# Linear attention and a swish layer on one core: the tail chunk moves from last place to last but one

## The chip, the cores and the metric

The kernel runs on one core of a Trainium2 chip. The core has five engines with instruction streams of their own: TensorE (PE, matrix products, with its weight loads shown as PEld), VectorE (DVE), ScalarE (ACT), GpSimd (POOL) and SyncE (SP, which here only issues transfers). Sixteen DMA engines move data between the memory outside the core (HBM) and the on-chip memory of 128 partitions. The metric is the device time of one execution in microseconds. Before the change it was 293.87 us, the median of three runs from 293.31 to 294.41.

## The reference, cut to what matters

```python
q_s = softmax(q, axis=-1)              # over the 64 elements of a head
k_s = softmax(k, axis=2)               # over the 576 tokens of a batch
kv  = einsum('bhsd,bhse->bhde', k_s, v)
x   = einsum('bhsd,bhde->bhse', q_s, kv)   # then (b, s) rows of h*d = 512
h   = x @ w_in                         # 4608x512 by 512x2048
g   = h * (1 / (1 + exp(-beta * h)))
out = g @ w_out                        # 4608x2048 by 2048x512, float32
```

There are 8 batches, 8 heads, 576 tokens and 64 elements per head. The two products of the second half are most of the arithmetic.

## The kernel before, in words

The 4608 rows are worked in nine chunks of 512 rows. Chunks 0 to 7 hold the first 512 tokens of each batch ("main"), four tokens in each partition. Chunk 8 (`c == B`) holds what is left, the last 64 tokens of all eight batches ("tail"); its partitions 0 to 63 belong to even batches and 64 to 127 to odd ones.

For each chunk a loop runs over `j`, the sixteen blocks of 128 columns of the hidden layer. `mm_a` (L309) makes one block of h with four products and lets ACT take a tanh (L326) and DVE form g (L328). `mm_b` (L340) multiplies g into four accumulators, one for each block `st` of 128 rows, with a lag of two blocks. The accumulators of a chunk are finished in the first two steps of the next chunk (`finish_b`, L431), where `store` (L356) copies them to a staging tile of four buffers (`wo`), ACT the even and DVE the odd ones, and issues the stores to HBM. A main chunk in mid-kernel is stored by two transfers on SP, each of two row blocks on all 128 partitions, 4 KB in a row (L378).

What the next chunk needs is prepared beside this one. `side(c, u)` (L538) is called at each step `u` and, for `b = c + 1`, emits q's exponential, sum and scaling (steps 2 to 5), k's exponential and v's cast (steps 4 to 6), the transpose of the scaled q by a DMA on SP (`q_xbar`, step 6, L235), the k-by-v products and their normalization (steps 8 and 10) and the products that make x (`x_mm`, steps 11 to 14). For a main chunk `x_mm` is one product of 512 columns for each of four head pairs; for the tail chunk it is eight products of 64 columns for each (L300). At step 9 `load_next` (L423) issues on SP the loads of the chunk after next: q (L80), k (L104, with its 64 tail tokens at L108) and v (likewise). The tail chunk needs only q, which `load_qtail` (L83) fetches with eight transfers of 64 partitions and 256-byte rows (L88).

The order on each engine is that of the program: the kernel is scheduled by hand. So SP's queue has, in each chunk, two stores, a transpose, and then the loads, and an instruction that waits holds what follows it.

In the last chunk the sixteenth block is drained in another order (L585 to L590): accumulators 0 and 1 are finished first, then 2, then 3, and each is stored as soon as it is ready. Because the last chunk is the tail, each store is cut in two halves of 64 partitions (`e` = 0 and 1): blocks 0 and 1 together by two transfers on SP, block 2 by two on ACT, block 3 by one on SP and one on ACT.

```python
(nc.scalar if st == 2 or (st == 3 and e) else nc.sync).dma_start(   # L367
```

Of the kernel before, what the change touches and what calls it, by code (L numbers as in the profile page):

```python
# [10 lines left out]
F32 = mybir.dt.float32  # L11
# [6 lines left out]
def kernel(  # L18
# [10 lines left out]
    nc = tc.nc  # L29
# [6 lines left out]
    NJ = FF // P  # L36
# [5 lines left out]
    NW = 2  # L42
    D1 = D + 1
    LAG = 2
    NCH = B + 1

    const = ctx.enter_context(tc.tile_pool(name="const", bufs=1))
    stage = ctx.enter_context(tc.tile_pool(name="stage", bufs=1))
# [26 lines left out]
    def load_q(b, parts=1):  # L75
        t = stage.tile([P, H, R * D], F32, tag="q_st", bufs=2, name=f"q_st{b}")
        src = q[b, :, 0:MAIN, :].rearrange("h (p i) d -> p h (i d)", i=R)
        n = H // parts
        for s in range(parts):
            nc.sync.dma_start(t[:, s * n : (s + 1) * n, :], src[:, s * n : (s + 1) * n, :])  # L80
        q_st[b] = t
# [12 lines left out]
    def load_kv(d, src, b, tag, parts=1):  # L94
        t = stage.tile([P, H * (R + 1) * D], F32, tag=tag, bufs=2, name=f"{tag}{b}")
        if b < NW:
            d[b] = t[:, 0 : HP * RW * D].rearrange("p (j r) -> p j r", j=HP)
            sv = src[b].rearrange("(j e) (p i) d -> (e p) j (i d)", e=2, i=RW)
            n = HP // parts
            for s in range(parts):  # L100
                nc.sync.dma_start(d[b][:, s * n : (s + 1) * n, :], sv[:, s * n : (s + 1) * n, :])
        else:
            d[b] = t[:].rearrange("p (h r) -> p h r", h=H)
            nc.sync.dma_start(  # L104
                d[b][:, :, 0 : R * D], src[b, :, 0:MAIN, :].rearrange("h (p i) d -> p h (i d)", i=R)
            )
            e = b % 2
            nc.sync.dma_start(  # L108
                d[b][e * TAIL : (e + 1) * TAIL, :, R * D : R * D + D],
                src[b, :, MAIN:S, :].rearrange("h t d -> t h d"),  # L110
            )
# [140 lines left out]
    def kv_mm(b, jj, n=2, tag="att"):  # L252
        t = ps.tile([P, n, 2 * D1], F32, tag=tag, bufs=2 if tag == "att" else 1, name=f"kv{b}_{jj}")
        att_of[b, jj] = t
        for jl in range(n):
            j = n * jj + jl
            if b < NW:
                for i in range(RW):
                    nc.tensor.matmul(
                        t[:, jl, 0:D1],  # L260
                        ek[b][:, j, i, :],
                        va[b][:, j, i, :],
                        start=(i == 0),
                        stop=(i == RW - 1),
                    )
                continue
            for i in range(R):
# [14 lines left out]

    def kv_norm(b, jj, n=2):
        t = att_of.pop((b, jj))
        rk = work.tile([P, n, 1], F32, tag="rk", bufs=2, name=f"rk{b}_{jj}")
        nc.vector.reciprocal(rk[:], t[:, :, D : D + 1])
        for e in range(2):
            r = slice(e * D, (e + 1) * D)
            dst = kvp[r, b, n * jj : n * jj + n, e * D : (e + 1) * D]
            src = t[r, :, 0:D] if b < NW else t[r, :, e * D1 : e * D1 + D]  # L290
# [49 lines left out]
    def mm_b(c, j, sts=range(R)):  # L340
        acc = acc_tiles(c)
        g = g_of[c, j]
        for st in sts:
            nc.tensor.matmul(  # L344
                acc[st][:],
                g[:, ds(st * P, P)],
                w_out_b[:, j, :],
                start=(j == 0),
                stop=(j == NJ - 1),
            )  # L350
# [5 lines left out]
    def store(c, st):  # L356
        acc = acc_of[c]
        eng = nc.scalar if st % 2 == 0 else nc.vector
        if c == B:
            lo, hi = ((0, 2), (0, 2), (2, 3), (3, 4))[st]  # L360
            if st == lo:
                o_of[c] = stage.tile([P, R, DM], F32, tag="wo", bufs=4, name=f"o{c}_{lo}")
            o = o_of[c]
            evac(eng, o[:, st, :], acc[st][:])
            if st == hi - 1:
                for e in range(2):
                    (nc.scalar if st == 2 or (st == 3 and e) else nc.sync).dma_start(  # L367
                        out_t[:, MAIN:S, :].rearrange("(i e) t f -> e t i f", e=2)[e, :, lo:hi, :],
                        o[e * TAIL : (e + 1) * TAIL, lo:hi, :],
                    )  # L370
            return
        if st == 0:
            o_of[c] = stage.tile([P, R, DM], F32, tag="wo", bufs=4, name=f"o{c}")
        o = o_of[c]
        evac(eng, o[:, st, :], acc[st][:])
        if st % 2 == 1:
            ov = out[c * S : c * S + MAIN, :].rearrange("(p i) f -> p i f", i=R)
            nc.sync.dma_start(ov[:, st - 1 : st + 1, :], o[:, st - 1 : st + 1, :])  # L378
# [41 lines left out]
    ek_buf(1, nc.gpsimd)  # L420
    v_buf(1)

    def load_next(nb):  # L423
        if nb < B:
            load_q(nb)
            load_kv(k_st, k, nb, "k_st")
            load_kv(v_st, v, nb, "v_st")
        elif nb == B:
            load_qtail()

    def finish_b(c, j):  # L431
        mm_b(c, j)
# [67 lines left out]
    pool_cast(("in", 3), ("out", 3))  # L500

    for u in range(4, NJ):
        mm_a(0, u)
# [7 lines left out]
        if u in (11, 13):  # L511
# [23 lines left out]
    mm_b(1, 0)  # L535
    mm_b(1, 1)

    def side(c, u):  # L538
        b = c + 1
        if b > B:  # L540
            return
        tail = b == B
        o = 2 if c == 1 else 0
        if u in (2 + o, 3 + o):
            q_exp(b, u - 2 - o)
            q_sum(b, u - 2 - o)
        if u in (4 + o, 5 + o):
            q_mul(b, u - 4 - o)
            if not tail:
                k_exp(b, u - 4 - o)  # L550
        if u == 4 + o and not tail:
            v_buf(b)
            v_cast(b, nc.gpsimd)
            vtail_cast(b, nc.gpsimd)
        if u == 6 + o:
            if not tail:
                ktail_exp(b)
            q_xbar(b)
        if u in (8 + o, 10 + o) and not tail:
            kv_mm(b, (u - 8 - o) // 2)  # L560
            kv_norm(b, (u - 8 - o) // 2)
        if 11 <= u < 15:
            j = u - 11
            x_mm(b, j, nc.scalar if j % 2 == 0 else nc.vector)
        if u == 9:
            load_next(c + 2)

    for u in range(4):
        side(1, u)
    for c in range(1, NCH):  # L570
        for j in range(4 if c == 1 else 0, NJ - 1 if c == B else NJ):
            lead = c > 1 and j == 3
            if not lead:
                mm_a(c, j)
            if c > 1 and j == 2:
                mm_a(c, 3)
            if (c, j) == (B, NJ - 2):
                pass
            elif j >= LAG:
                mm_b(c, j - LAG)  # L580
            else:
                finish_b(c - 1, NJ + j - LAG)
            side(c, j)
    mm_a(B, NJ - 1, tag="att")
    last = [(0, j) for j in range(NJ - 4, NJ - 1)] + [(1, j) for j in range(NJ - 4, NJ - 1)]  # L585
    last += [(0, NJ - 1), (1, NJ - 1)] + [(st, j) for st in (2, 3) for j in range(NJ - 4, NJ)]
    for st, j in last:
        mm_b(B, j, [st])
        if j == NJ - 1:
            store(B, st)  # L590
# [1 line left out]
_INS = ['q', 'k', 'v', 'moe_w_in', 'moe_w_out', 'moe_beta']  # L592
_OUTS = [((4608, 512), 'float32')]
# [25 lines left out]
```

The softmax here doesn't subtract the row's maximum and nothing guards it: scores larger than these inputs give would overflow.

## Time and profile before

| What | Value |
|---|---|
| Median of three runs | 293.87 us |
| The profiled execution's own time | 294.54 us |
| Its span, first to last instruction | 292.4 us |
| PE busy | 279.5 us, 96% |
| DVE busy | 184.2 us, 63% |
| ACT busy | 163.9 us, 56% |
| POOL busy | 42.0 us, 14% |
| Granted TensorE clock | 0.996 |

The profile is one execution. Its span leaves out 2.1 us of the execution's own time, which lie before the first or after the last instruction. Lines of the timeline read: start in us from the span's start, duration in us, engine, source line, operation, output and inputs, number of instructions merged. A trailing q on an engine's name (SPq, ACTq) means that the engine's queue was issuing a transfer. "To landing" is the time from the issue of a transfer to the arrival of its last byte as the profile sees it. The lines of the stretch views give the stretch, its length, the busy time and instruction count of PE, PEld, DVE, ACT and POOL, the granted clock, the mean busy share of the sixteen DMA engines, and the GB/s that they moved.

### The profile page before, as it was taken

How to read it: one execution, taken by the hardware profiler on the slowest of the kernel's cores; microseconds unless marked ns; L12 is line 12 of the kernel's file. 1: busy time of each engine (PE TensorE's matmuls, PEld its weight loads, DVE VectorE, ACT ScalarE, POOL GpSimd, SP SyncE). 2: the span in 40 equal slices, each digit the busy share in tenths (PEclk: the TensorE clock that was granted, in tenths of full speed). 3: DMA queues.
4: the chain of work that ended last, by engine and by line, in shares of the span. 5: the costliest groups of instructions: out<-in, count | busy, mean ns of one | idle time of the engine just before them, and what ended most of it. 6: DMA issues, size and time to landing. Idle time of an engine off the chain costs nothing.

```text
span 292.4 us, 3879 instructions
## 1 busy us (share of the span) xinstructions
PE 279.5 (96%) x1447; PEld 131.0 (45%) x1475; DVE 184.2 (63%) x299; ACT 163.9 (56%) x238; POOL 42.0 (14%) x55
## 2 busy tenths in 40 slices
PE   8898979999999999999999999999999999999991
PEld 3443435445444444454445444544454444544440
DVE  7853696695578557855695469456954694563441
ACT  4863666684486448734773567346825654453340
POOL 4539670300030021002100110003000000000000
PEclk9999999999999999999999999999999999999998
DMA  7999999708932963297319821981293023012005
GB/s 243 378 385 371 377 385 311 248 2 233 296 152 62 315 162 123 62 326 177 123 40 302 223 90 54 303 234 64 84 165 52 32 115 72 0 58 87 0 0 144
DMA packets 55971, 50.06 MB, mean 171 GB/s; under 512 B 26241, under 2 KB 47761, under 8 KB 55953
## 3 DMA queue, kind: packets, MB, share of 16 engines
q1 hardware_dynamic: 55712, 49.43, 55.8%
q10 hardware_dynamic: 240, 0.39, 0.5%
q8 instruction: 11, 0.18, 0.3%
q14 instruction: 8, 0.06, 0.1%
HBM read 36.71 MB, written 9.44 MB: 158 GB/s over the span
## 4 chain that ended last, share of the span: by engine, by line
PE 85%; DMA 6%; DVE 2%; ACT 1%; issue 1%; SPq 1%; another core or an unknown queue 1%; POOL 0%; ACTq 0%
DMA w_out_100<-in_moe_w_out_dram 4%; DMA v_st_91<-in_v_dram 2%; PE acc_3_724 L344 1%; PE acc_2_2458 L344 1%; PE acc_0_2456 L344 1%; PE acc_3_2459 L344 1%; PE acc_1_2167 L344 1%; PE acc_1_1300 L344 1%; PE acc_1_1589 L344 1%; PE acc_1_2728 L344 1%; PE acc_1_1011 L344 1%; PE acc_1_722 L344 1%; PE acc_1_1878 L344 1%; PE acc_2_1879 L344 1%; PE acc_2_1590 L344 1%; PE acc_0_721 L344 1%
## 5 line engine op out<-in xcount | busy, mean ns | idle before, releaser
L316 PEld LDWEIGHTS <-w_in_b 128*128 128x128 bf16 x576 | 55.3, 98 | 65.5 <-issue 2.7
L386 PEld LDWEIGHTS <-kvp 128*128 128x128 bf16 x34 | 3.7, 117 | 6.2 <-issue 3.6
L140 POOL CAST va_2202<-v_st_2007 128x2048 bf16<-128x2048 f32 x1 | 1.9, 1919 | 29.5 <-DMA v_st_2007<-in_v_dram 29.5
L140 POOL CAST va_1913<-v_st_1718 128x2048 bf16<-128x2048 f32 x1 | 1.9, 1918 | 26.7 <-DMA v_st_1718<-in_v_dram 26.7
L140 POOL CAST va_1624<-v_st_1429 128x2048 bf16<-128x2048 f32 x1 | 1.9, 1922 | 26.6 <-DMA v_st_1429<-in_v_dram 26.6
L153 ACT ACTIVATE ek_144<-k_st_86 64x576 bf16<-64x576 f32 x8 | 5.5, 681 | 0.2
L153 ACT ACTIVATE ek_149<-k_st_118 64x576 bf16<-64x576 f32 x8 | 5.4, 676 | 0.0
L140 POOL CAST va_1046<-v_st_836 128x2048 bf16<-128x2048 f32 x1 | 1.9, 1920 | 24.0 <-DMA v_st_836<-in_v_dram 24.0
L140 POOL CAST va_1335<-v_st_1140 128x2048 bf16<-128x2048 f32 x1 | 1.9, 1917 | 22.7 <-DMA v_st_1140<-in_v_dram 22.7
L296 PEld LDWEIGHTS <-kvp 128*128 128x128 bf16 x32 | 3.1, 98 | 4.2 <-DVE kvp L291 1.0
L140 POOL CAST va_147<-v_st_91 128x576 bf16<-128x576 f32 x4 | 3.3, 860 | 6.3 <-DMA v_st_91<-in_v_dram 6.3
L209 ACT ACTIVATE eq_189<-q_st_83 128x1024 bf16<-128x1024 f32 x2 | 2.1, 1056 | 3.0 <-DMA q_st_83<-in_q_dram 3.0
L140 POOL CAST va_783<-v_st_132 128x2048 bf16<-128x2048 f32 x1 | 1.9, 1916 | 12.2 <-DMA v_st_132<-in_v_dram 12.2
L140 POOL CAST w_in_b<-w_in_114 128x1024 bf16<-128x1024 f32 x2 | 3.0, 1536 | 2.1 <-DMA w_in_114<-in_moe_w_in_dram 2.1
L226 DVE TENSOR_TENSOR eq_485<-eq_485,rq_487 128x1024 bf16<-128x1024 bf16 x2 | 3.3, 1652 | 0.0
L140 POOL CAST w_out_b<-w_out_100 128x1024 bf16<-128x1024 f32 x2 | 2.4, 1205 | 4.6 <-DMA w_out_100<-in_moe_w_out_dram 4.6
L140 POOL CAST w_out_b<-w_out_116 128x1024 bf16<-128x1024 f32 x2 | 2.6, 1292 | 1.7 <-DMA w_out_116<-in_moe_w_out_dram 1.7
L220 DVE TENSOR_REDUCE rq_191<-eq_189 128x16 f32<-128x1024 bf16 x2 | 2.4, 1215 | 0.3 <-ACT eq_189 L209 0.3
L220 DVE TENSOR_REDUCE rq_487<-eq_485 128x16 f32<-128x1024 bf16 x2 | 2.4, 1212 | 0.3 <-ACT eq_485 L209 0.3
L220 DVE TENSOR_REDUCE rq_748<-eq_746 128x16 f32<-128x1024 bf16 x2 | 2.4, 1212 | 0.3 <-ACT eq_746 L209 0.3
L220 DVE TENSOR_REDUCE rq_1887<-eq_1885 128x16 f32<-128x1024 bf16 x2 | 2.4, 1191 | 0.3 <-ACT eq_1885 L209 0.3
L220 DVE TENSOR_REDUCE rq_2176<-eq_2174 128x16 f32<-128x1024 bf16 x2 | 2.4, 1190 | 0.3 <-ACT eq_2174 L209 0.3
(1461 smaller groups left out, 838.9 us busy)
## 6 DMA issues: line engine op xcount, KB each, us to landing
k_st_86<-in_k_dram SPq DMA_DIRECT2D x4, 288.0 KB, 5.7
v_st_91<-in_v_dram SPq DMA_DIRECT2D x4, 288.0 KB, 6.5
k_st_118<-in_k_dram SPq DMA_DIRECT2D x4, 288.0 KB, 9.6
v_st_124<-in_v_dram SPq DMA_DIRECT2D x2, 576.0 KB, 9.3
q_st_83<-in_q_dram SPq DMA_DIRECT2D x2, 512.0 KB, 4.3
w_in_97<-in_moe_w_in_dram SPq DMA_DIRECT2D x2, 512.0 KB, 6.4
w_out_100<-in_moe_w_out_dram SPq DMA_DIRECT2D x2, 512.0 KB, 9.3
w_in_102<-in_moe_w_in_dram SPq DMA_DIRECT2D x1, 1024.0 KB, 9.3
```

Of the source, the lines that this page charges most:

```text
L140: eng.tensor_copy(dst, src)
L153: nc.scalar.activation(ek[b][r, j : j + m, :, e * D : (e + 1) * D], k_st[b][r, j : j + m, :].rearrange("p j (i d) -> p j i d", i=RW), ACTF ...
L209: nc.scalar.activation(eq[b][:, :, s * m : (s + 1) * m, :].rearrange("p i h d -> p h i d"), q_st[b][:, s * m : (s + 1) * m, :].rearrange(" ...
L220: nc.vector.tensor_reduce(rq[b][:, 0, :, h], eq[b][:, :, h, :], axis=AX.X, op=ALU.add)
L226: nc.vector.tensor_tensor(eq[b][:, :, h, :], eq[b][:, :, h, :], rq[b][:, 1, :, h].unsqueeze(3).to_broadcast((P, R, m, D)), ALU.mult,)
L296: nc.tensor.matmul(t[:], kvp[:, c, j, :], qsT[c][:, :, j, :])
L316: nc.tensor.matmul(h[:], w_in_b[:, kt, ds(j * P, P)], x_of(c)[:, kt, :], start=(kt == 0), stop=(kt == KT - 1),)
L344: nc.tensor.matmul(acc[st][:], g[:, ds(st * P, P)], w_out_b[:, j, :], start=(j == 0), stop=(j == NJ - 1),)
L386: nc.tensor.matmul(t[:, 0:cols], kvp[:, B - 1, 0, :], kvp[:, B - 1, :, :].rearrange("p j r -> p (j r)")[:, 0:cols],)
```

## The change

The chunks get an explicit order. With `LASTMAIN` set, the tail chunk runs in the eighth place and the main chunk of batch 7 in the ninth. `side` now takes a place `n`: q and x are prepared for the chunk in place n + 1, k and v still for batch n + 1. So in place 6 (chunk 6) the tail's q is worked together with k and v of batch 7, and in place 7 (the tail chunk) q of batch 7 is worked alone. `load_next` follows: the tail's eight loads are issued in place 5, ahead of k and v of batch 7, and q of batch 7 in place 6. The tail chunk is stored in mid-kernel by four transfers of 64 partitions on SP. The last chunk, now a main one, uses four staging tiles and four stores of 128 partitions and one row block each: blocks 0, 2 and 3 on SP, block 1 on ACT. Two other switches of the new text, `FIX` and `COLT`, are off.

```diff
-    NCH = B + 1
+    FIX, LASTMAIN, COLT = False, True, False
+    NCH = B + 1
+    order = list(range(NCH))
+    if LASTMAIN:
+        order[B - 1], order[B] = B, B - 1
+    LASTC = order[-1]
...
     def store(c, st):
         acc = acc_of[c]
         eng = nc.scalar if st % 2 == 0 else nc.vector
+        if c == B and c != LASTC:
+            if st == 0:
+                o_of[c] = stage.tile([P, R, DM], F32, tag="wo", bufs=4, name=f"o{c}")
+            o = o_of[c]
+            evac(eng, o[:, st, :], acc[st][:])
+            if st % 2 == 1:
+                for e in range(2):
+                    nc.sync.dma_start(
+                        out_t[:, MAIN:S, :].rearrange("(i e) t f -> e t i f", e=2)[e, :, st - 1 : st + 1, :],
+                        o[e * TAIL : (e + 1) * TAIL, st - 1 : st + 1, :],
+                    )
+            return
...
+        if c == LASTC:
+            o = stage.tile([P, R, DM], F32, tag="wo", bufs=4, name=f"o{c}_{st}")
+            evac(eng, o[:, st, :], acc[st][:])
+            ov = out[c * S : c * S + MAIN, :].rearrange("(p i) f -> p i f", i=R)
+            (nc.sync, nc.scalar, nc.sync, nc.sync)[st].dma_start(ov[:, st, :], o[:, st, :])
+            return
...
-    def load_next(nb):
-        if nb < B:
-            load_q(nb)
-            load_kv(k_st, k, nb, "k_st")
-            load_kv(v_st, v, nb, "v_st")
-        elif nb == B:
+    def load_next(n):
+        if order[n] < B:
+            load_q(order[n])
+        else:
             load_qtail()
+        if n < B:
+            load_kv(k_st, k, n, "k_st")
+            load_kv(v_st, v, n, "v_st")
...
-    def side(c, u):
-        b = c + 1
-        if b > B:
+    def side(n, u):
+        if n + 1 >= NCH:
             return
-        tail = b == B
+        qc = order[n + 1]
+        kb = n + 1
...
-            q_exp(b, u - 2 - o)
-            q_sum(b, u - 2 - o)
+            q_exp(qc, u - 2 - o)
+            q_sum(qc, u - 2 - o)
...
-            x_mm(b, j, nc.scalar if j % 2 == 0 else nc.vector)
-        if u == 9:
-            load_next(c + 2)
+            x_mm(qc, j, nc.scalar if j % 2 == 0 else nc.vector)
+        if u == 9 and n + 2 < NCH:
+            load_next(n + 2)
...
-    for c in range(1, NCH):
-        for j in range(4 if c == 1 else 0, NJ - 1 if c == B else NJ):
+    for n in range(1, NCH):
+        c = order[n]
+        for j in range(4 if n == 1 else 0, NJ - 1 if n == B else NJ):
...
-        mm_b(B, j, [st])
+        mm_b(LASTC, j, [st])
         if j == NJ - 1:
-            store(B, st)
+            store(LASTC, st)
```

More of the change, by code (lines that the diff above doesn't have):

```diff
@@ L266, in kv_mm @@
                 continue
+            if COLT:
+                for i in range(R + 1):
+                    for e in range(2):
+                        hd = 2 * j + e
+                        nc.tensor.matmul(
+                            t[e * D : (e + 1) * D, jl, 0:D1],
+                            ek[b][:, i, hd, :] if i < R else ekt[(b // 2) % 2][:, ds(hd * D, D)],
+                            va[b][:, i, hd, :] if i < R else vt[(b // 2) % 2][:, b % 2, hd, :],
+                            start=(i == 0),
+                            stop=(i == R),
+                            tile_position=(0, e * D),
+                        )
+                continue
             for i in range(R):
@@ L289, in kv_norm @@
             dst = kvp[r, b, n * jj : n * jj + n, e * D : (e + 1) * D]
-            src = t[r, :, 0:D] if b < NW else t[r, :, e * D1 : e * D1 + D]
+            src = t[r, :, 0:D] if b < NW or COLT else t[r, :, e * D1 : e * D1 + D]
             nc.vector.tensor_tensor(dst, src, rk[r].to_broadcast((D, n, D)), ALU.mult)
@@ L358, in store @@
         eng = nc.scalar if st % 2 == 0 else nc.vector
+        if c == B and c != LASTC:
[4 more added lines that the diff above has]
+            if st % 2 == 1:
+                for e in range(2):
+                    nc.sync.dma_start(
+                        out_t[:, MAIN:S, :].rearrange("(i e) t f -> e t i f", e=2)[e, :, st - 1 : st + 1, :],
+                        o[e * TAIL : (e + 1) * TAIL, st - 1 : st + 1, :],
+                    )
+            return
         if c == B:
@@ L366, in store @@
                 for e in range(2):
-                    (nc.scalar if st == 2 or (st == 3 and e) else nc.sync).dma_start(
+                    if FIX:
+                        q_eng = (nc.sync, nc.sync, nc.gpsimd, nc.scalar if e else nc.sync)[st]
+                    else:
+                        q_eng = nc.scalar if st == 2 or (st == 3 and e) else nc.sync
+                    q_eng.dma_start(
                         out_t[:, MAIN:S, :].rearrange("(i e) t f -> e t i f", e=2)[e, :, lo:hi, :],
@@ L421 @@
     v_buf(1)
-    def load_next(nb):
-        if nb < B:
-            load_q(nb)
-            load_kv(k_st, k, nb, "k_st")
-            load_kv(v_st, v, nb, "v_st")
-        elif nb == B:
+    def load_next(n):
+        if order[n] < B:
+            load_q(order[n])
+        else:
             load_qtail()
+        if n < B:
+            load_kv(k_st, k, n, "k_st")
+            load_kv(v_st, v, n, "v_st")
     def finish_b(c, j):
@@ L502 @@
     for u in range(4, NJ):
-        mm_a(0, u)
+        if not (FIX and u == 5):
+            mm_a(0, u)
+        if FIX and u == 4:
+            mm_a(0, 5)
+            mm_b(0, 2)
+            continue
+        if FIX and u in (12, 14):
+            for j in (u - 12, u - 11):
+                q_pet(1, j, nc.scalar if u == 12 else nc.vector)
         mm_b(0, u - LAG)
@@ L510 @@
             q_mul(1, (u - 10) // 2)
-        if u in (11, 13):
+        if not FIX and u in (11, 13):
             for j in (u - 11, u - 10):
@@ L536 @@
     mm_b(1, 1)
-    def side(c, u):
-        b = c + 1
-        if b > B:
+    def side(n, u):
+        if n + 1 >= NCH:
             return
-        tail = b == B
-        o = 2 if c == 1 else 0
+        qc = order[n + 1]
+        kb = n + 1
+        o = 2 if n == 1 else 0
         if u in (2 + o, 3 + o):
-            q_exp(b, u - 2 - o)
-            q_sum(b, u - 2 - o)
+            q_exp(qc, u - 2 - o)
+            q_sum(qc, u - 2 - o)
         if u in (4 + o, 5 + o):
[L548 to L554, printed above, removed]
-        if u == 6 + o:
[L556 to L561, printed above, removed]
+            q_mul(qc, u - 4 - o)
+            if kb < B:
+                k_exp(kb, u - 4 - o)
+        if u == 4 + o and kb < B:
+            v_buf(kb)
+            v_cast(kb, nc.gpsimd)
+            vtail_cast(kb, nc.gpsimd)
+        if u == 6 + o:
+            if kb < B:
+                ktail_exp(kb)
+            q_xbar(qc)
+        if u in (8 + o, 10 + o) and kb < B:
+            kv_mm(kb, (u - 8 - o) // 2)
+            kv_norm(kb, (u - 8 - o) // 2)
         if 11 <= u < 15:
             j = u - 11
-            x_mm(b, j, nc.scalar if j % 2 == 0 else nc.vector)
-        if u == 9:
-            load_next(c + 2)
+            x_mm(qc, j, nc.scalar if j % 2 == 0 else nc.vector)
+        if u == 9 and n + 2 < NCH:
+            load_next(n + 2)
     for u in range(4):
         side(1, u)
-    for c in range(1, NCH):
-        for j in range(4 if c == 1 else 0, NJ - 1 if c == B else NJ):
-            lead = c > 1 and j == 3
-            if not lead:
+    for n in range(1, NCH):
+        c = order[n]
+        for j in range(4 if n == 1 else 0, NJ - 1 if n == B else NJ):
+            if not (n > 1 and j == 3):
                 mm_a(c, j)
-            if c > 1 and j == 2:
+            if n > 1 and j == 2:
                 mm_a(c, 3)
-            if (c, j) == (B, NJ - 2):
+            if (n, j) == (B, NJ - 2):
                 pass
@@ L581 @@
             else:
-                finish_b(c - 1, NJ + j - LAG)
-            side(c, j)
-    mm_a(B, NJ - 1, tag="att")
+                finish_b(order[n - 1], NJ + j - LAG)
+            side(n, j)
+    mm_a(LASTC, NJ - 1, tag="att")
     last = [(0, j) for j in range(NJ - 4, NJ - 1)] + [(1, j) for j in range(NJ - 4, NJ - 1)]
```

## The prediction

> **What bounds the kernel now.** I read the page's busy shares first, then the work by stretches of the last chunks, then the timeline of the last 8 us, then SP's own timeline around the tail's loads. Busy shares, and two stretches (chunk 6, chunk 7):
>
> ```profile
> PE 279.5 (96%) x1447; PEld 131.0 (45%) x1475; DVE 184.2 (63%) x299; ACT 163.9 (56%) x238; POOL 42.0 (14%) x55
> ...
> 202.80:232.60 29.80, 29.64 (x150) 13.98 (x152) 19.57 (x33) 17.55 (x26) 0.00 (x0) 1.00 0.45 89
> 232.60:261.30 28.70, 28.54 (x158) 13.42 (x160) 18.03 (x27) 15.00 (x23) 0.00 (x0) 1.00 0.17 55
> ```
>
> PE is busy 29.64 of 29.80 us and 28.54 of 28.70 us: from chunk 2 on the kernel is a row of matrix products without gaps, and whatever is prepared beside them costs nothing while it is in time. Chunk 7 is shorter because no k and v follow it. This ends at 286.27 us. The timeline of the end, transfers and copies alone, and the stretches in which the DMA engines drain (the two last columns are their busy share and GB/s; the first line is the store of chunk 7 in mid-kernel, for comparison):
>
> ```profile
> 284.58 0.69 DVE L140 COPY o_0_2894<-acc_1_2728 128x512 f32<-128x512 f32 x1 [0.70 <-PE acc_1_2728 L344]
> ...
> 285.34 1.34 SPq L367 DMA_DIRECT2D out_dram<-o_0_2894  x2
> ...
> 285.45 0.58 ACT L138 COPY o_2_2904<-acc_2_2729 128x512 f32<-128x512 f32 x1 [0.49 <-PE acc_2_2729 L344]
> ...
> 286.06 1.31 ACTq L367 DMA_DIRECT2D out_dram<-o_2_2904  x2
> 286.31 0.69 DVE L140 COPY o_3_2912<-acc_3_2730 128x512 f32<-128x512 f32 x1 [1.03 <-PE acc_3_2730 L344]
> 287.03 0.95 SPq L367 DMA_DIRECT2D out_dram<-o_3_2912  x1
> 287.47 1.76 ACTq L367 DMA_DIRECT2D out_dram<-o_3_2912  x1
> ```
>
> ```profile
> 263.00:263.60 0.60, 0.60 (x5) 0.29 (x3) 0.16 (x1) 0.00 (x0) 0.00 (x0) 1.00 0.99 396
> 286.60:288.60 2.00, 0.00 (x0) 0.00 (x0) 0.40 (x1) 0.00 (x0) 0.00 (x0) 1.00 0.91 189
> 288.60:291.00 2.40, 0.00 (x0) 0.00 (x0) 0.00 (x0) 0.00 (x0) 0.00 (x0) 0.83 0.91 276
> ```
>
> So 6.1 us, from 286.27 to 292.4, hold no computation but a copy of 0.69: the last 1 MB (four row blocks of 256 KB) is written. The engines are 91% busy but move 189 and then 276 GB/s, where the mid-kernel store moves 396. The list of issues gives 4.0 us to landing for the last half block, so it lands at 287.47 + 4.0 = 291.47; the span ends 0.93 later. SP around the tail's loads in the kernel before:
>
> ```profile
> 183.28 0.57 SPq L80 DMA_DIRECT2D q_st_2002<-in_q_dram  x1
> 183.90 0.70 SPq L104 DMA_DIRECT2D k_st_2004<-in_k_dram  x1
> ...
> 187.68 4.32 SPq L108 DMA_DIRECT2D v_st_2007<-in_v_dram  x1
> ...
> 213.06 6.26 SPq L88 DMA_DIRECT2D q_st_tail<-in_q_dram  x8
> ```
>
> **What the Trainium skill says.** "SBUF — State Buffer", section "Door 1: The DMA port swizzle (why `[64,N]` ≈ `[32,N]`)": partitions 0 to 63, or 64 to 127, reach half of the 16 DMA ports, 196 GB/s at 1 MiB against 328 for all 128. The trace agrees: 189 GB/s in the first 2 us, when mostly half-width stores are in flight, 396 for stores of 128 partitions. "DMA: Bandwidth & Descriptors", section "Rules for kernel authors": two transfers to disjoint halves serialize, use one of 128 partitions. The 276 GB/s of the later stretch, with both halves in flight on two queues, lies between. "Perfetto Trace Analysis", section "DMA Optimizations": transfers below 2 KB carry much overhead, and going from 2 KB to 4 KB helps. The mid-kernel stores have 4 KB rows, both versions of the last stores 2 KB rows; no run here separates row length from width yet.
>
> **The change part by part.** *PE.* No product is added. The tail's x moves from chunk 7 to chunk 6; eight products of 64 columns take 0.23 us (250.50 to 250.73), one of 512 takes 0.21 (221.83 to 222.04), so chunk 6 grows and the eighth place shrinks by 4 x 0.02. Sum 0. The tail's x needs kvp of batch 7, normalized at steps 8 and 10; main chunks need theirs at the same steps, so it is no new wait.
>
> *ACT and DVE.* The tail's q tile has the shape of a main one; two exponentials of 1.05 us, two sums of 1.2, two scalings of 1.2 trade places with equals. Sum 0. The tail's q exponential now waits for eight transfers, not one.
>
> *Loads.* Chunk 5 issues at 183.28 the eight tail loads (6.26 us of issue instead of q's 0.57) ahead of k and v of batch 7. In the kernel before the engines are saturated by these loads and the transpose ahead of them from 213 to 222, 9.0 us. Laid at 183.3, that ends at 192.3. Before, q, k and v land from 183.3 to 198.8, 15.5 us for 3.26 MB, of which q is 4.7 us; so k and v need 10.8 and land by about 203.1, 4.3 us later. Who waits: POOL's cast of v (starts at 198.79 on landing; 1.92, and 0.61 for its tail) then ends at 205.6, and the first k-by-v product runs at 213.57: 8.0 us of cover. k's exponential starts at 206.43; k lands at 183.90 + 10.5 + 4.3 = 198.7: 7.7 us. The tail's q lands near 193 for an exponential at 203.84. Behind the loads in SP's queue stand the stores of chunk 5 (202.74); issue of v ends at 187.68 + 4.32 + 5.7 = 197.7. Each transfer takes the next of eight completion semaphores and waits for the transfer eight before it: k waits for the first tail load, which lands 3.7 after its issue, inside the 6.26. The transpose ahead of the loads takes 5.1 us beside tail loads instead of 3.7; it was so before in chunk 6, with its user at 219.9, 3.4 us after landing. In chunk 6 only q of batch 7 is loaded, near 213, for an exponential near 233.6. All of this costs 0; without the cover it would cost up to 4.3 us.
>
> *Mid-kernel store of the tail.* Four half-width transfers instead of two, near 261: perhaps 4 us of drain instead of 2.6, with nothing behind them for 24 us. Cost 0.
>
> *The end.* Block 0's copy ends on ACT at 284.95 and SP issues at once, not at 285.34. Block 1's copy ends at 285.27 and ACT issues at 285.34. ACT works in order, so block 2's copy, ready at 285.41 and started at 285.45 before, stands behind that issue. An issue takes 0.34 (mid-kernel stores) to 0.69 (ACT's at the end): the copy runs from about 285.7 to 286.05, plus 0.58, and SP issues block 2 at 286.3 to 286.65 for 0.34 to 0.67. SP is free for block 3 at 286.7 to 287.35; its copy ends at 287.00. So block 3's issue comes at 287.05 to 287.4, I take 287.2. To landing: a mid-kernel store of 512 KB with nothing ahead lands in 2.8 us, 1.3 of it transfer at 396 GB/s; half the bytes save 0.65, so 2.15 at best. At worst 3.2, the first half-width store of 256 KB at the end (the shorter of two). I take 2.6, above the floor by 0.45 for 2 KB rows and block 2 just ahead. Landing 289.8, plus 0.93: span 290.7, a gain of 1.7. Ends: 287.05 + 2.15 + 0.93 = 290.1, gain 2.3; 287.4 + 3.2 + 0.93 = 291.5, gain 0.9.
>
> The sum is 0 + 0 + 0 + 0 - 1.7 against the profiled span of 292.4 (execution 294.54). The median of the runs is 0.67 below that execution; I take the difference from the median: 293.87 - 1.7 = 292.2 us, its own range 291.4 to 292.9.
>
> **The rivals.** *A, the drain keeps its rate.* If 2 KB rows and not half width limit the stores, 1 MB drains in the same 4.4 us and only starts 0.4 earlier (284.97 against 285.34): 293.5 us. For it: both versions write 2 KB rows. Against it: the rate rises to 276 GB/s within the same kernel when both halves are in flight.
>
> *B, k or v of batch 7 come too late (slower).* Place: ACT's exponential of k in chunk 6 at 206.43, with the tanh of that chunk behind it and PE behind the tanh. It decides once k lands over 7.7 us later than worked out, so 12 us later than before. From there each us costs one; it passes the gain of 1.7 at 9.4 us. A delay of 11 us too many gives 293.87 - 1.7 + 3.3 = 295.5 us. For it: 256-byte rows keep the engines full for 9 us and move only 165 GB/s, and SP's v issue already took 4.32 us under back pressure. Against it: the shift is worked out from the same transfers at 4.3 us, little over half the cover.
>
> *C, ACT's issue of block 1 holds block 2.* If it takes 1.76 us, as ACT's last one did, block 2's copy ends at 287.7, SP issues it at 287.7 and block 3 at 288.35; with 2.6 the span ends at 291.9: 293.4 us. For it: that row. Against it: at 285.34 the engines are idle, and ACT's first two issues took 0.59 and 0.69.
>
> *That the change does not act* is excluded: transfers of 128 partitions at the end are in the order written out.
>
> **How the numbers follow.** Forecast 0.62, A 0.15, C 0.11, B 0.12. The bound of 0.5% is 1.5 us, about what a measurement of this kernel can tell from no change (its runs spread over 1.1). Of the forecast's range 0.9 to 2.3 some three quarters of the chance lie past 1.5: faster 0.48, and 0.14 within. A, C and a fifth of B stay within: same 0.42. B's rest: slower 0.10. The range goes from 291.3 (the best end) to 293.9, which takes in A and C and leaves out B and a little on both sides, some 2 in 10.
>
> **What would show it.** In chunk 6 to the ninth place PE must stay busy without a gap; POOL's last cast starts near 203; k's exponential near 206.4. At the end block 3's issue stands near 287.2, lands within 3 us, and the drain moves over 350 GB/s; A shows 200 to 280 GB/s there, C shows block 2's copy after 287. The prediction is wrong if the last issue comes after 288, if its landing still takes 4 us, or if PE shows an idle time in chunk 6 released by ACT or POOL.

## The result and the profile after

The changed kernel took 291.43 us, the median of six runs (290.83 to 292.26), against 294.14 us for the kernel before, run beside it six times (293.31 to 294.73). The ratio is 0.9912 with a 95% interval from 0.9887 to 0.9938: 2.7 us faster, clear of the noise. The forecast was 292.2 us, a gain of 1.7. The profiled execution took 292.26 us with a span of 290.5 us, 1.9 us shorter than the span before.

The page's busy times after, and the stretches of chunk 6 and of the eighth place:

```profile
PE 278.6 (96%) x1447; PEld 131.0 (45%) x1475; DVE 185.2 (64%) x299; ACT 163.9 (56%) x238; POOL 41.5 (14%) x55
```

```profile
202.80:232.65 29.85, 29.69 (x179) 14.57 (x180) 19.55 (x33) 17.53 (x26) 0.00 (x0) 1.00 0.33 89
232.65:261.30 28.65, 28.49 (x131) 12.90 (x132) 18.05 (x27) 15.01 (x23) 0.00 (x0) 1.00 0.18 55
```

PE is as full as before in both places; chunk 6 grew by 0.05 us and the eighth place shrank by as much. The last matrix product begins at 285.92 us, before it was 285.89. So all 1.9 us lie behind it. The timeline of the end, copies and issues alone, then one stretch of the drain, then the list of issues (KB of one transfer, us to landing):

```profile
285.00 0.35 SPq L410 DMA_DIRECT2D out_dram<-o_0_2896  x1
...
285.33 0.37 ACTq L410 DMA_DIRECT2D out_dram<-o_1_2900  x1
...
285.80 0.58 ACT L143 COPY o_2_2907<-acc_2_2731 128x512 f32<-128x512 f32 x1 [0.82 <-PE acc_2_2731 L362]
...
286.34 0.69 DVE L145 COPY o_3_2914<-acc_3_2732 128x512 f32<-128x512 f32 x1 [1.03 <-PE acc_3_2732 L362]
286.41 0.34 SPq L410 DMA_DIRECT2D out_dram<-o_2_2907  x1
287.06 0.33 SPq L410 DMA_DIRECT2D out_dram<-o_3_2914  x1
```

```profile
286.20:288.60 2.40, 0.10 (x1) 0.00 (x0) 0.69 (x1) 0.18 (x1) 0.00 (x0) 1.00 1.01 367
```

```profile
out_dram<-o_3_2914 SPq DMA_DIRECT2D x1, 256.0 KB, 2.5
```

Block 3's issue stands at 287.06 us and lands 2.5 later, at 289.56; with the same 0.93 to the end as before this makes 290.5. The DMA engines drain 367 GB/s where they drained 189 and then 276. An issue costs 0.33 to 0.37 us where an issue of half the partitions cost 0.59 to 0.95 and once 1.76.

The moved loads, on SP, and POOL's cast that waits for v of batch 7:

```profile
183.31 6.40 SPq L93 DMA_DIRECT2D q_st_tail<-in_q_dram  x8
189.75 0.63 SPq L109 DMA_DIRECT2D k_st_2011<-in_k_dram  x1
...
191.12 0.57 SPq L109 DMA_DIRECT2D v_st_2014<-in_v_dram  x1
```

```profile
200.18 1.92 POOL L145 CAST va_2209<-v_st_2014 128x2048 bf16<-128x2048 f32 x1 [29.12 <-DMA v_st_2014<-in_v_dram]
```

The cast starts 1.4 us later than before (198.79), and the product that needs it still runs at 213.6.

The first four experiments ran beside 35 runs of the kernel before with a median of 294.04 us. Two intervals serve below as measures that do not depend on how the first part of a run went. (There the runs differ: the 201st matrix product begins between 41.4 and 42.6 us in the traces. From it to chunk 5's transpose all kernels take the same 139.0 us.) The *end stretch* runs from the start of block 3's copy to the end of the span: 292.4 - 286.31 = 6.09 us before, 290.5 - 286.34 = 4.16 us after. The *body* runs from the issue of chunk 5's transpose on SP to the start of block 3's copy: 286.31 - 181.56 = 104.75 us before, 286.34 - 181.58 = 104.76 us after. Spans are given to a tenth of a microsecond, so an end stretch is known to about 0.05.

### The profile page after: what moved, and what is told of

The parts are those of the page before. It is cut to its first block, busy times and chain, and to the rows that moved or that the text cites. A ratio compares the mean times of both kernels' runs of the same rounds, so it can differ in the third digit from the quotient of the medians.

```text
span 290.5 us, 3880 instructions
## 1 busy us (share of the span) xinstructions
PE 278.6 (96%) x1447; PEld 131.0 (45%) x1475; DVE 185.2 (64%) x299; ACT 163.9 (56%) x238; POOL 41.5 (14%) x55
## 4 chain that ended last, share of the span: by engine, by line
PE 87%; DMA 4%; DVE 3%; ACT 1%; issue 1%; another core or an unknown queue 1%; SPq 0%; POOL 0%; ACTq 0%
DMA k_st_86<-in_k_dram 2%; DMA w_in_97<-in_moe_w_in_dram 2%; PE acc_2_2486 L362 1%; PE acc_0_2173 L362 1%; PE acc_3_724 L362 1%; PE acc_2_2731 L362 1%; PE acc_0_2484 L362 1%; PE acc_2_2175 L362 1%; PE acc_2_1879 L362 1%; PE acc_0_1877 L362 1%; PE acc_1_1589 L362 1%; PE acc_3_2176 L362 1%; PE acc_0_1588 L362 1%; PE acc_2_1012 L362 1%; PE acc_0_1010 L362 1%; PE acc_0_721 L362 1%
## 5 line engine op out<-in xcount | busy, mean ns | idle before, releaser
L145 POOL CAST va_147<-v_st_91 128x576 bf16<-128x576 f32 x4 | 2.7, 668 | 7.8 <-DMA v_st_91<-in_v_dram 7.6
L334 PE MATMUL h_0_316<-xT_80,w_in_b 128*128 128x512 bf16 x4 | 1.5, 380 | 1.5 <-POOL w_in_b L145 1.3
L145 DVE CAST w_in_b<-w_in_102 128x1024 bf16<-128x1024 f32 x2 | 2.6, 1312 | 0.0
L225 DVE TENSOR_REDUCE rq_748<-eq_746 128x16 f32<-128x1024 bf16 x2 | 2.4, 1214 | 0.3 <-ACT eq_746 L214 0.3
L225 DVE TENSOR_REDUCE rq_487<-eq_485 128x16 f32<-128x1024 bf16 x2 | 2.4, 1213 | 0.3 <-ACT eq_485 L214 0.3
L225 DVE TENSOR_REDUCE rq_191<-eq_189 128x16 f32<-128x1024 bf16 x2 | 2.4, 1215 | 0.2 <-ACT eq_189 L214 0.2
```

The lines of the kernel that those rows point to most:

```text
L145: eng.tensor_copy(dst, src)
L225: nc.vector.tensor_reduce(rq[b][:, 0, :, h], eq[b][:, :, h, :], axis=AX.X, op=ALU.add)
L334: nc.tensor.matmul(h[:], w_in_b[:, kt, ds(j * P, P)], x_of(c)[:, kt, :], start=(kt == 0), stop=(kt == KT - 1),)
```

## The experiments

**Half the partitions, nothing else.** Each of the four last stores becomes two of 64 partitions, on the same queue.

```diff
-            (nc.sync, nc.scalar, nc.sync, nc.sync)[st].dma_start(ov[:, st, :], o[:, st, :])
+            for e in range(2):
+                r = slice(e * TAIL, (e + 1) * TAIL)
+                (nc.sync, nc.scalar, nc.sync, nc.sync)[st].dma_start(ov[r, st, :], o[r, st, :])
```

> The changed kernel, with each of its four last stores cut into two of 64 partitions on the same queue; rows stay 2 KB, order of chunks as changed. End stretch here means: from the start of block 3's copy to the end of the span; it was 6.09 us before and 4.16 us after. Theory (width and what comes with it: issues of 0.6 us instead of 0.35, half the drain rate): the gain is gone, end stretch 6.0 to 7.5 us, since eight issues of 0.6 us now stand in line on SP and ACT; time 293.9 to 295.5 us. Rival A (2 KB rows limit the drain, earlier issue brought the gain): end stretch 4.2 to 4.6 us, time about 291.6 us.

The median was 293.49 us beside 294.04 before, ratio 0.9986 (0.9977 to 0.9996). The span was 292.2 us; its timeline at the end and a stretch of the drain:

```profile
284.78 4.64 SPq L412 DMA_DIRECT2D out_dram<-o  x6
285.11 1.19 ACTq L412 DMA_DIRECT2D out_dram<-o  x2
286.11 0.69 DVE L145 COPY o<-acc 128x512 f32<-128x512 f32 x1 [1.03 <-PE acc L362]
286.40 0.58 ACT L143 COPY o<-acc 128x512 f32<-128x512 f32 x1 [1.64 <-PE acc L362]
```

```profile
287.80:290.60 2.80, 0.00 (x0) 0.00 (x0) 0.00 (x0) 0.00 (x0) 0.00 (x0) 0.65 0.86 206
```

The last two issues of SP, and in the list of issues the last one (KB, us to landing):

```profile
288.22 1.20 SPq L412 DMA_DIRECT2D out_dram<-o  x2
```

```profile
out_dram<-o SPq DMA_DIRECT2D x1, 128.0 KB, 2.4
```

The end stretch is 292.2 - 286.11 = 6.09 us, as long as before. The rows are still 2 KB, and the first store leaves as early as in the changed kernel (284.78, 1.33 us ahead of block 3's copy; there 285.00, 1.34 ahead). So the width, with the issues that it multiplies, is what the gain rests on: the theory's figure, at its lower edge. The time was 0.4 us below the range expected.

That the length is the same as before looks like chance, for the time is lost in another place. Here the last half of block 3 is issued at about 288.8 us, 2.7 after the start of block 3's copy (0.72 in the changed kernel), and lands 2.4 later, as soon as the whole store did. All of the loss lies ahead of that last issue: six issues stand in line on SP, and the two on ACT, 1.19 us, push block 2's copy to 286.40, past block 3's. In the kernel before the last issue came 1.16 us after the copy's start (287.47 - 286.31) and landed 4.0 later: 0.4 us of its loss lie ahead of the issue, 1.5 behind it, in a drain with the DMA engines 91% busy. The 206 GB/s of this run are therefore no clean measure of the drain: SP hands out 128 KB in 0.60 us, by these figures an estimate of 218 GB/s. Whether the drain alone would have cost as much here stays open.

**The same stores with the tail last.** Only the order of the chunks differs from the run above.

```diff
-    FIX, LASTMAIN, COLT = False, True, False
+    FIX, LASTMAIN, COLT = False, False, False
...
-            lo, hi = ((0, 2), (0, 2), (2, 3), (3, 4))[st]
+            lo, hi = st, st + 1
...
-                        q_eng = nc.scalar if st == 2 or (st == 3 and e) else nc.sync
+                        q_eng = nc.scalar if st == 1 else nc.sync
```

> The order of chunks of the kernel before (tail last), with its last stores on the queues and in the blocks of the run with half-width stores and the main chunk last: two transfers of 64 partitions for each row block, blocks 0, 2, 3 on SP and 1 on ACT. It differs from that run in the order of the chunks alone. Theory (order by itself costs and brings nothing): end stretch within 0.3 us of that run, last matrix product within 0.3 us of the same time after chunk 2's start, time within 0.5 us. Rival (moving loads and work between chunks is itself worth something, which would explain why the medians moved by 2.7 us where the profile's end moved by 1.9): this kernel 0.8 us slower than that run.

The median was 293.95 us, ratio 1.0002 (0.9988 to 1.0016). Its copy of block 3:

```profile
285.98 0.69 DVE L145 COPY o<-acc 128x512 f32<-128x512 f32 x1 [1.03 <-PE acc L362]
```

End stretch 292.1 - 285.98 = 6.12 us against 6.09, body 104.76 against 104.75. The order of the chunks by itself moves nothing inside the span. Yet this kernel's median is 0.46 us above the other's. The spans, median over the runs of each, are 291.8 and 291.7 us; the rest lies outside the span, which the last experiments take up.

**Full width, the queues of before.** The stores are whole. In the program blocks 0 and 1 are both issued on SP after block 1's copy, as before, block 2 on ACT and block 3 on SP.

```diff
-            (nc.sync, nc.scalar, nc.sync, nc.sync)[st].dma_start(ov[:, st, :], o[:, st, :])
+            o_of[c, st] = o
+            for s in ((), (0, 1), (2,), (3,))[st]:
+                (nc.scalar if st == 2 else nc.sync).dma_start(ov[:, s, :], o_of[c, s][:, s, :])
```

> The changed kernel with full-width stores, but issued as before: blocks 0 and 1 both on SP after block 1's copy, block 2 on ACT, block 3 on SP. Theory (width alone): block 3 is still issued at about 287.05 and the drain is fast enough to have emptied the rest, end stretch 4.1 to 4.5 us, time 291.4 to 291.8 us. Rival (the earlier issue brought part of the gain): end stretch 4.6 to 5.2 us, time over 292 us.

The median was 291.57 us, ratio 0.9913 (0.9893 to 0.9933), the changed kernel's. The copies of blocks 1 and 3 and the issues, and the drain:

```profile
284.22 0.69 DVE L145 COPY o<-acc 128x512 f32<-128x512 f32 x1 [0.70 <-PE acc L362]
...
284.62 2.38 SPq L412 DMA_DIRECT2D out_dram<-o  x3
...
285.70 0.37 ACTq L412 DMA_DIRECT2D out_dram<-o  x1
285.95 0.69 DVE L145 COPY o<-acc 128x512 f32<-128x512 f32 x1 [1.04 <-PE acc L362]
```

```profile
286.20:288.20 2.00, 0.00 (x0) 0.00 (x0) 0.44 (x1) 0.00 (x0) 0.00 (x0) 1.00 1.03 367
```

(The first line of issues merges three with the waits between them.) End stretch 290.1 - 285.95 = 4.15 us. But the edit did not hold block 0 back. Its store left at 284.62, before block 1's copy ended (284.22 + 0.69 = 284.91) and 1.33 us ahead of block 3's copy, as early as in the changed kernel: each block has a staging tile of its own here, and SP waited for block 0's alone. What differs is mainly which queues take blocks 1 and 2, and that is worth nothing. The rival of the earlier issue is not tested by this run; the one above and the one below bear on it.

**Two stores of 4 KB rows.** Blocks 0 and 1 leave together, then blocks 2 and 3.

```diff
+            if st % 2 == 1:
+                nc.sync.dma_start(ov[:, st - 1 : st + 1, :], o[:, st - 1 : st + 1, :])
```

> The changed kernel with two last stores of 4 KB rows (blocks 0 and 1, blocks 2 and 3), as the mid-kernel stores are, both on SP. Theory (width, not row length): drain rate as with 2 KB rows, 350 to 400 GB/s; the last store carries 512 KB and lands 2.8 us after its issue instead of 2.5: end stretch 4.4 to 4.6 us, time 291.6 to 291.9 us. Rival A (row length): the drain is clearly faster than the 350 to 380 GB/s of the changed kernel, over 395 GB/s, and the end stretch no longer than 4.2 us in spite of twice the bytes.

The median was 292.08 us, ratio 0.9934 (0.9913 to 0.9956). Its two issues and block 3's copy, a stretch in which its engines are full, and the last store in the list of issues:

```profile
285.52 2.06 SPq L413 DMA_DIRECT2D out_dram<-o  x2
...
286.49 0.69 DVE L145 COPY o<-acc 128x512 f32<-128x512 f32 x1 [1.03 <-PE acc L362]
```

```profile
288.20:289.00 0.80, 0.00 (x0) 0.00 (x0) 0.00 (x0) 0.00 (x0) 0.00 (x0) 1.00 0.99 410
```

```profile
out_dram<-o SPq DMA_DIRECT2D x1, 512.0 KB, 2.6
```

Row length does count: 410 GB/s against 367, some 12%, which the theory had at nothing. The width counts for more: 367 against the 189 and then 276 GB/s of the kernel before, with the same 2 KB rows. The end stretch was 4.31 us, between the two expectations: twice the bytes hang on the last store, yet it landed 2.6 us after its issue, little later than the 2.5 of the changed kernel, where block 2's store was still under way. Rival A is right about the direction and explains a small part of the drain, not the gain. The time was 0.2 us above the theory's range, with 0.35 us more outside the span than the changed kernel had (see below).

This run also bears on the earlier issue. The first store leaves 0.97 us ahead of block 3's copy, as in the kernel before (286.31 - 285.34), and the end stretch is only 0.15 us longer than that of the changed kernel. With the half-width run, which left early and gained nothing, this says that the early issue is not what the gain rests on. How much it is worth with 2 KB rows is not shown.

**No issue on ACT.** Block 1's store goes to SP (`nc.sync` for all four).

> The changed kernel with block 1's store on SP instead of ACT, so that no issue stands ahead of block 2's copy on ACT. Theory (the last landing sets the end, block 3's issue waits only for its own copy): block 2's copy starts near 285.45 instead of 285.80, block 3 is still issued at its copy's end plus 0.05, end stretch 4.1 to 4.3 us against 4.16, time 291.2 to 291.7 us. Rival C (ACT's issue holds the end back): end stretch shorter by 0.3 us or more.

The median was 291.17 us beside 293.54 before, ratio 0.9911 (0.9877 to 0.9946).

```profile
284.37 0.58 ACT L143 COPY o<-acc 128x512 f32<-128x512 f32 x1 [0.49 <-PE acc L362]
...
285.23 0.69 DVE L145 COPY o<-acc 128x512 f32<-128x512 f32 x1 [1.04 <-PE acc L362]
```

Block 2's copy began after 0.49 us of idle time of ACT instead of 0.82; block 3's copy began at 285.23 and the span ended at 289.4: 4.17 us. Rival C's wait is there, 0.33 us long, and costs nothing, because block 3's issue waits for its own copy.

**The moved loads made two and three times as long.** The eight loads of the tail's q are repeated in place, so k and v of batch 7 stand behind 16 transfers; a second run has a third `*range(B)`, 24 transfers.

```diff
-        for b in range(B):
+        for b in [*range(B), *range(B)]:
```

> The changed kernel with the eight tail loads of q issued twice over, the second time to the same place, so that k and v of batch 7 come later by another set. In the changed kernel k landed at 196.2 and v at 200.2; a set costs 6.4 us of issue and up to 9 us of transfer, so k is expected at 202.5 to 205 and v at 206.5 to 209, for users at 206.4 and (by way of 2.5 us of casts) 213.6. Theory (the moved loads are hidden, with room): no idle time of PE in chunk 6, time within 0.3 us of the changed kernel's 291.4. Rival B (the loads were close to costing): PE idle in chunk 6 and over 1 us longer.

> The changed kernel with the tail loads of q issued three times over. k is expected at 209 to 213 for its user at 206.4. Theory (cover of some 10 us, then each us costs one): PE idle in chunk 6, released by ACT, 3 to 7 us longer than the changed kernel: 294.5 to 298.5 us. If the waits for k and v were not on a path that can set the end, the time stays near 291.4 us.

Medians 292.07 us (ratio 0.9942, 0.9919 to 0.9965) and 292.22 us (0.9943, 0.9924 to 0.9963), beside 293.54 before, in runs with a wide spread, so the profile has to speak. First SP's queue and POOL's cast of v with two sets; then, with three, that cast, the waits of PE from chunk 5 on and one of ACT in chunk 6 (engine, line, what it waited for, us in total, times, longest):

```profile
182.86 11.51 SPq L93 DMA_DIRECT2D q_st_tail<-in_q_dram  x16
194.42 0.63 SPq L109 DMA_DIRECT2D k_st<-in_k_dram  x1
...
205.41 1.92 POOL L145 CAST va<-v_st 128x2048 bf16<-128x2048 f32 x1 [34.48 <-DMA v_st<-in_v_dram]
```

```profile
211.40 1.92 POOL L145 CAST va<-v_st 128x2048 bf16<-128x2048 f32 x1 [41.06 <-DMA v_st<-in_v_dram]
```

```profile
PE kv L293 <- POOL vt L208: 0.3, 1, 0.3
PE kv L286 <- POOL va L145: 0.2, 1, 0.2
```

```profile
ACT ek L169 <- DMA k_st<-in_k_dram: 1.5, 1, 1.5
```

A second set costs 5.1 us of issue. POOL's cast of v starts 24.3 us after the issue of chunk 5's transpose instead of 18.6 (205.41 - 181.15 and 200.18 - 181.58), PE waits for nothing new, and the body is 285.93 - 181.15 = 104.78 us: hidden. (The median is 0.6 us above the changed kernel's 291.43, outside the 0.3 expected; the trace shows nothing of that from chunk 5 on.) With three sets ACT waits 1.5 us for k, v is cast after 30.7 us (211.40 - 180.69), and the body is 286.56 - 180.69 = 105.87 us: 1.1 us longer. Product by product against the changed kernel, PE falls behind by all of this 1.1 us between 207 and 214 us: by some 0.3 before the k-by-v products, after ACT's late exponential of k, and by the rest at these products, which wait for POOL's casts of v. So late loads are on a path that can set the end, as rival B had it, though the larger part comes by way of v's cast and not of k's exponential, the place that B named. A set costs less than expected, and the cover is not used up by the change: it takes more than one further set to reach it. The 3 to 7 us expected of the third set were too many for the same reason.

**Block 3's copy shared by two engines.** DVE copies one half of the columns, ACT the other, each half is stored at once, 1 KB rows.

```diff
+            if st == 3:
+                for x, (ce, de) in enumerate(((nc.vector, nc.sync), (nc.scalar, nc.scalar))):
+                    f = slice(x * 256, (x + 1) * 256)
+                    evac(ce, o[:, st, f], acc[st][:, f])
+                    de.dma_start(ov[:, st, f], o[:, st, f])
+                return
```

> The changed kernel with block 3's copy cut into two halves of 256 columns, one on DVE and one on ACT, each stored by its own engine pair (SP and ACT) with 1 KB rows. Theory (the end is copy, issue, landing in a row): both halves are copied by about 286.75 instead of 287.03 and issued at about 286.8; if a store of 1 KB rows lands in 2.5 us as the 256 KB store did, the end stretch is 3.8 to 3.95 us and the time about 291.1. Rival A in another form (short rows slow the store): landing 2.9 us or more, and nothing is gained.

```profile
286.06 0.42 DVE L145 COPY o<-acc 128x256 f32<-128x256 f32 x1 [1.03 <-PE acc L362]
286.52 0.37 ACT L143 COPY o<-acc 128x256 f32<-128x256 f32 x1 [0.41 <-DVE o L145]
```

The halves ran one after the other: ACT's waited 0.41 us for DVE's, a dependence between the two writers of one tile. The second half was issued at 286.93, 0.87 us after block 3's copy began, where the whole block is issued after 0.72. End stretch 290.4 - 286.06 = 4.34 us, median 292.16 us beside 293.54 (ratio 0.9941, 0.9915 to 0.9968). The edit did not do what it was to test, so whether two halves side by side would help was not tried.

**The time outside the span.** Each run has a time and a span. Their difference, median over the runs of a kernel, was 2.15 us for the kernel before, for the tail-last half stores and for the 4 KB pairs, and 1.78 to 1.81 us for the changed kernel and the others, whatever their stores. The one count that went along was the number of instructions in DVE's program, waits included: 319 in the three, 320 in the rest. (The traces record two fewer in every kernel, 317 and 318.) One memset of a column of its own, early on DVE, changes the count alone:

```diff
+    extra = const.tile([P, 1], F32, name="extra")
+    nc.vector.memset(extra[:], 0.0)
```

> The kernel before with one more instruction on DVE, a memset of one column of a tile of its own in the first microseconds, whose 0.1 us no one waits for. The time outside the span (a run's time less its span) was 2.15 us in the kernel before and in the two experiments whose programs hold 319 instructions on DVE, waits included, and 1.80 us in the changed kernel and the six experiments that hold 320. If the number of DVE's instructions goes with it, this kernel (320) shows 1.80 us outside the span, and a time 0.35 us shorter than before with the same span. If the order of the chunks or the last stores set it, it stays at 2.15 us and the time is that of before.

> The changed kernel with the same extra memset on DVE: 321 instructions. If an exact count of 320 (or a multiple of some block) is what matters, the time outside the span goes from 1.80 back to about 2.15 us or to another value, and the time up by 0.35; if more than 319 is enough, or if the last stores set it, it stays at 1.80 us. The span is that of the changed kernel, end stretch 4.1 to 4.2 us.

The kernel before with 320 instructions had 1.81 us outside its span, the changed kernel with 321 had 1.88. So the 0.35 us go with the count and have nothing to do with chunks or stores. The medians were 293.95 us (ratio 0.9997, 0.9982 to 1.0012) and 291.53 us (0.9929, 0.9906 to 0.9953), beside 293.69 before. The first did not get shorter as a whole: its spans had a median of 292.15 us against 291.5 beside it, and the expectation of an equal span missed. (The kernel before alone had medians of 291.9, 291.4 and 291.5 in the three series.) Why the count matters, and whether the time lies ahead of the first instruction or behind the last, stays open.

**Block 3 copied by ACT.** All stores on SP, block 2's copy on DVE and block 3's on ACT; then the same with the extra memset.

```diff
-            evac(eng, o[:, st, :], acc[st][:])
+            evac((nc.scalar, nc.vector, nc.vector, nc.scalar)[st], o[:, st, :], acc[st][:])
```

> The changed kernel with all four last stores on SP and the last two copies exchanged: block 2 on DVE, block 3 on ACT, whose copy of this size takes 0.58 instead of 0.69 us. The copy of block 3 should end 0.1 us earlier and the end stretch be 4.0 to 4.1 us. Its program holds 319 instructions on DVE; if their number sets the time outside the span, that is 2.15 us, and the time about 291.6 us in spite of the shorter end.

> The kernel of the run with block 3's copy on ACT, with one more memset on DVE, 320 instructions. The end stretch is the same, 4.0 to 4.1 us; if the number of DVE's instructions sets it, the time outside the span is 1.80 us and the time 0.1 us below that of the changed kernel, about 291.2 us.

Medians 291.90 us (ratio 0.9935, 0.9916 to 0.9954) with 319 instructions and 2.15 us outside the span, and 291.58 us (0.9924, 0.9903 to 0.9945) with 320 and 1.77: the count's effect a third time, between two kernels whose spans differ by 0.05 us. Block 3's copy took 0.59 us, but the end stretches are 290.2 - 286.10 = 4.10 and 290.2 - 286.03 = 4.17 us. The 0.1 us was not found again at the end, and neither kernel beats the changed one.

## Why the prediction was right, and where its sizes were off

*PE: nothing added.* Right. The body is 104.75 and 104.76 us, and the tail's x cost chunk 6 0.05 us.

*ACT and DVE: equals trade places.* Right; no new wait of PE.

*Loads: hidden.* Right in the verdict, mis-sized in the term. k and v were to come 4.3 us later, v's cast to start near 203. k came 1.7 later (194.4 to 189.75 + 6.3 = 196.1) and v 1.4. The 9.0 us for the tail set were about right: its last load landed at 192.7, where 192.3 was foretold. The mis-sized term is the 10.8 us that k and v were to need from there. v's cast started 7.5 us after it. k had been issued 3 us before the set was in, and q's share of the 15.5 us, put at 4.7, was 5.9 in the kernel before (issue to landing), which leaves 9.6 for k and v instead of 10.8. The DMA engines were 84% busy from 183.3 to 189.6, so during the set they were not full; that points to the issue, 6.4 us for the first set and 5.1 for a further one, as what sets the pace there. Rival B was a real path, but two more sets were needed to make it cost 1.1 us.

*Mid-kernel store of the tail: 0.* Right; issued from 261.26 us for 3.37 us, with nothing behind it on SP until 285.

*The end: -1.7.* Right in every step and 0.2 short in the sum. Block 3's issue at 287.2 came at 287.06, since with issues of 0.34 us, the lower bound, SP was free before block 3's copy ended at 287.03. The 2.6 to landing were 2.5. Span 290.7 foretold, 290.5 measured. That the half width is the cause was shown by cutting the width alone: 6.09 us again, though there it is lost ahead of the last issue and not, as before, mostly in the drain. The Trainium skill, "SBUF — State Buffer", section "Door 1: The DMA port swizzle (why `[64,N]` ≈ `[32,N]`)", has 196 against 328 GB/s for 64 and 128 partitions at 1 MiB; the kernel before drained 189 GB/s and then 276, the changed kernel 367. The prediction put the first rate down to half-width stores and the second to both halves in flight. But all six of those stores are half-width, and both halves had been issued on both queues by 286.7. The landings tell more: the first store of each queue, from partitions 0 to 63, landed 3.2 us after its issue, the second 4.4 to 4.6. So it is likely that in the first stretch one half drained from both queues, and that in the second the two halves drained together, faster than one alone and slower than whole stores; they did not simply serialize, which the prediction had cited. The earlier issue, which the sum carried along, was not separated from the width, but the runs leave it a small part at most.

*The bridge to the median.* Here the forecast fell short: 1.7 foretold, 2.7 measured. 1.93 us are the end stretch (6.09 - 4.16). 0.35 us are outside the span (2.15 to 1.80), tied to DVE's instruction count, which went from 319 to 320 with the change; the prediction carried the time outside the span over unchanged, and no view shown before the change told of it. The remaining 0.4 us can lie only in the first part of the runs, if these went as the traces did: there the spans of one kernel differ by 1.5 us (289.0 to 290.5 for the changed one). Beside the later runs of kernels with the same end the difference of the spans was 1.9 to 2.1, so I take these 0.4 for scatter, which is argued and not shown.

*The rivals.* A: row length is worth 12% of the drain rate, not the gain. C: the wait on ACT exists and is covered. B: the path is real and was far off; see the loads.

## What to carry to other kernels

What comes last should be written by transfers of all 128 partitions: the same last 1 MB in halves of 64 drained at 189 to 276 instead of 367 GB/s, each half cost an issue of about 0.6 us where a whole block cost 0.35, and nothing covers either behind the last product. So the order of independent pieces may be chosen by the shape of the last one's store, as long as the loads that this moves still land ahead of their users. Before a gain in the last microseconds is put down to a change, look at time less span as well: an instruction more or less moved it by 0.35 us.

## What the runs showed that was not expected

- The time outside the span went with the number of instructions on DVE: 319 gave 2.15 us in four kernels (the one before among them), 320 gave 1.77 to 1.81 in nine, 321 gave 1.88 in one. Two pairs of kernels, 319 against 320, differ in nothing but an idle memset.
- An issue of a store of 64 partitions held its queue for about 0.6 us, one of 128 partitions and the same rows for 0.33 to 0.38, though it carries twice the rows.
- Two ways of losing gave the same end stretch of 6.1 us: in the kernel before mostly the drain, with half-width stores and the main chunk last the issues in line ahead of the last one.
- A repeated set of eight loads of 256-byte rows cost 5.1 us of issue on SP, the next one 5.5, and what stood behind it moved by little more than that: v's cast by 5.7 us with the second set and by 6.5 with the third.
